# Score pairs in neighbouring PSUM banks, and a new written-out order, in a fused attention and gated-MLP kernel

## The chip, the cores and the metric

The kernel runs on one core of a Trainium2 chip. The metric is the device time of one execution in microseconds (us). Before the change the median of three runs is 380.63 us (377.94 to 382.38). The engines are called PE (TensorE; PEld is its weight load), ACT (ScalarE), DVE (VectorE), POOL (GpSimd) and SP (SyncE, which only issues DMAs here).

## The reference

```
q, k, v: (8 batches, 12 heads, 448 positions, 64)
q_n, k_n = q / rms(q) * g_q, k / rms(k) * g_k          # rms over the 64
attn     = softmax(q_n @ k_n^T / 8)
x        = (attn @ v), heads side by side              # (8, 448, 768)
h        = relu(x @ w_in)                              # 768 -> 1024
u, vv    = h[..., :512], h[..., 512:]
v_n      = (vv - mean(vv)) / sqrt(var(vv) + 1e-6)      # over the 512
v_s      = w_spatial @ v_n + b_spatial                 # mixes the 448 positions
out      = (u * v_s) @ w_out                           # 512 -> 768
```

## The kernel before

The work of one batch is split into three groups of four heads, 24 groups G in all; batch b has the groups 3b to 3b+2. The 448 positions are taken as 7 chunks of 64. Everything is one stream of words in a string `PLAN`; a loop at the end calls for each word the function `op_<letter>`. The order of the words is the order of the instructions on every engine: each engine runs its own instructions in that order and waits by semaphores, which the framework derives from the tiles that instructions read and write. A word has arguments, then after a slash its buffers or banks, then the engine (a ACT, v DVE, g POOL). So `S.13.5/03` computes scores of group 13, unit 5, into banks 0 and 3; `S.13.6/17` unit 6 into banks 1 and 7; `V.3.0.0/2` starts block 0 of batch 3 in bank 2, and `V.3.2.0/6` block 2 in bank 6. All of PSUM is one tile `ps` of 8 banks.

The words, with the lines of the kernel before:

- L, l load raw q or k (SP; l, q, r, i, j, n, p, k are the forms of group 0, cut in halves r so that work starts early); Q squares (L361 POOL or DVE, L359 ACT), R sums (L372, L378), I and J take ln and exp for the reciprocal root (L385, L390; L395, L398), N and n normalise (L404, L412).
- P and p transpose on PE (L426, L435), K and k evict to the tiles qT and kT (L342, L340; kT scaled by the gains, L449 DVE, L447 ACT); T transposes q by DMA instead (L464).
- S computes a pair of score tiles, two banks (L506). E takes exp of both in one ACT instruction into a tile `et` (L514); there are 7 S and 7 E for each group, 168 in all.
- s, a, b are column passes over the `et` tiles (L539): sums of the exps, and the two halves of attn @ v. D and d give the reciprocal sums (L554, L558 ACT), X multiplies into `xt` (L564 DVE).
- V and U are the two halves of x @ w_in (L580, L651); c and u are their relus (L573 DVE, L571 ACT); B takes the statistics (L616, L617), M, m, w prepare them (L622, L625 ACT, L630 DVE), A normalises (L639 ACT); H mixes positions (L665), G multiplies (L670 DVE), O is the output product (L679), W the tails of V and O (L604), o evicts (L342, L340), t writes out (SP, L696).
- v loads v (L290, L293), wi, ws, wo load weights w_in, w_sp, w_out (L300, L304, L307), all on POOL's queue; wb loads the bias on SP (L311). z.44 puts 44 dummy matmuls (L260). gA, gB, gC make the column of gains (L346, L351, L354).

The exp reads its two banks as one stepped slice:

```
act.activation(out=ets[sl[0]], in_=ps[:, a:b + 1:b - a, 0:S], func=AF.Exp, bias=0.0, scale=1.0)
```

In the plan before, b − a is 1 for 40 of the 168 pairs, 2 for 48, and 3 to 7 for 80.

Of the kernel before, what the change touches and what calls it, by code (L numbers as in the profile page):

```python
# [20 lines left out]
l.1.0/0 setup//v l.0.0/1 l.1.1 l.0.1 L.1.0/2 L.1.1/3 L.2.1/4 gA//v L.4.0/5 gB/0 z.44/7 L.2.0/6 q.1.0/0/a r.1.0//v  # L21
q.0.0/1/a r.0.0//v i.0//a j.0//a q.1.1//a q.0.1//g r.1.1//v n.0.0/0/g gC//v r.0.1//v Q.1.0/2/a n.1.0/1/v p.0.0/1
i.1//a p.1.0/2 R.1.0//v j.1//a z.17/7 n.1.1//g Q.1.1/0/a k.0.0/0/v n.0.1//g k.1.0/0/a p.1.1/3 L.3.1/0 R.1.1//v z.8/7
wi.1.0//g L.3.0/1 S.0.0/45 k.1.1//v I.1//a S.0.1/67 J.1//a E.0.0/0/a p.0.1/0 N.1.0/2/v S.0.2/12 E.0.1/1/a N.1.1/3/v
P.1.0/3 L.4.1/2 k.0.1//a z.8/5 K.1.0/1/v Q.2.0/2/g P.1.1/4 L.5.1/3 Q.2.1/1/a z.15/7 K.1.1/1/v E.0.2/2/a R.2.1//v
S.1.0/56 S.1.2/07 v.0.1//g S.0.3/34 E.1.2/3/a S.1.1/12 R.2.0//v v.0.0//g E.1.1/4/a S.1.4/07 Q.3.0/0/v v.0.2//g I.2//a
J.2//a E.1.4/5/a N.2.0/1/v v.0.3//g E.1.0/6/a N.2.1/0/v P.2.0/1 L.5.0/6 E.0.3/7/a S.0.5/02 K.2.0/2/v Q.4.0/1/g
S.1.6/57 E.0.5/8/a P.2.1/6 S.1.3/34 K.2.1/2/v E.1.6/9/a S.0.4/02 z.4/1 Q.3.1/2/v wi.0.1//g E.1.3/a/a S.1.5/57 S.0.6/16
E.1.5/b/a wi.0.3//g s.1.0/3 R.3.1//v a.1.0/4 E.0.6/c/a wi.1.2//g S.2.4/57 R.3.0//v a.1.1 s.1.1 E.2.4/d/a S.2.1/16
s.1.2 R.4.0//v Q.4.1/2/g E.0.4/e/a s.1.3 s.0.0/5 a.0.0/7 I.3//a a.0.1 J.3//a s.0.1 E.2.1/f/a wi.0.2//g s.0.2 R.4.1//v  # L30
s.0.3 D.1/0/a a.0.2 wi.0.0//g S.2.3/02 D.0/1/a N.3.0/2/v S.2.0/16 b.0.0/3 d.0//a b.1.0/5 b.0.1 wi.1.3//g E.2.3/g/a
N.3.1/3/v b.0.2 b.0.3 wi.1.1//g E.2.0/h/a S.2.6/02 X.0.1//v a.0.3 a.1.2 I.4//a X.0.0//v P.3.0/1 J.4//a E.2.6/0/a
N.4.0/1/g S.2.5/36 K.3.0/3/v P.3.1/7 E.2.5/7/a s.2.0/0 K.3.1/3/v a.1.3 S.2.2/12 d.1//a b.1.1 a.2.0/3 Q.5.0/0/g
E.2.2/4/a T.4.0/1 S.3.1/67 b.1.2 E.3.1/6/a b.1.3 S.3.4/12 X.1.1//v a.2.1 E.3.4/1/a L.6.1/4 Q.5.1/1/g X.1.0//v a.2.2
L.7.0/1 S.3.0/67 s.2.1 L.6.0/0 E.3.0/e/a S.3.2/15 b.2.0/4 s.2.2 E.3.2/2/a N.4.1/0/g R.5.1//v s.2.3 S.3.3/26 D.2/1/a
b.2.1 a.2.3 R.5.0//v b.2.2 E.3.3/8/a b.2.3 S.3.6/17 d.2//a S.3.5/05 I.5//a P.4.1/2 X.2.0//v J.5//a V.0.1.0/6 E.3.6/c/a
N.5.0/2/g K.4.1/1/v U.0.3.0/3 E.3.5/3/a V.0.1.1 X.2.1//v U.0.3.1 V.0.1.2 ws//g T.5.0/0 S.4.5/17 c.0.1//v S.4.1/24
E.4.5/a/a W.0/0 N.5.1/3/g B.0.1//v E.4.1/5/a L.7.1/5 S.4.3/56 wb c.0.3//v S.4.4/17 S.4.0/24 E.4.3/b/a U.0.3.2
U.0.2.0/0 Q.7.0/2/a u.0.3//v V.0.0.0/5 B.0.3//v U.0.0.0/6 E.4.4/9/a P.5.1/3 Q.6.0/0/g V.0.0.1 R.7.0//v E.4.0/f/a
U.0.1.0/1 U.0.0.1 Q.6.1/1/a K.5.1/0/v V.0.0.2 v.1.1//g U.0.2.1 c.0.0//a R.6.1//v S.5.2/27 v.1.0//g S.5.3/34 E.5.2/h/a  # L40
U.0.1.1 V.0.2.0/5 R.6.0//v E.5.3/4/a U.0.0.2 V.0.2.1 I.6//a U.0.1.2 J.6//a Q.7.1/2/a V.0.2.2 N.6.0/0/g u.0.1//v
U.0.2.2 u.0.0//v S.5.4/27 S.4.2/34 u.0.2//v E.5.4/g/a Y.1/1 c.0.2//v Y.2/6 v.1.3//g T.6.0/2 E.4.2/7/a R.7.1//v
S.4.6/02 s.3.0/7 N.6.1/1/g E.4.6/d/a s.4.0/5 S.5.0/34 y.2//v s.4.1 L.10.1/2 I.7//a s.3.1 y.1//v s.4.2 J.7//a L.9.0/6
s.3.2 E.5.0/0/a B.0.2//v s.4.3 L.9.1/3 S.5.1/02 v.1.2//g S.5.5/16 D.4/0/a s.3.3 B.0.0//v a.3.0/3 b.3.0/4 D.3/1/a
N.7.0/3/g a.3.1 b.3.1 E.5.5/6/a Y.3/5 P.6.1/7 y.3//v E.5.1/e/a S.5.6/16 K.6.1/2/v Y.0/5 T.7.0/3 M.0//a d.3//a s.5.0/0
y.0//v m.0//a a.5.0/2 E.5.6/2/a b.3.2 w.0//v b.4.0/7 wx//v a.3.2 b.3.3 d.4//a s.5.1 L.8.0/0 a.4.0/5 X.3.1//v A.0.3//a
L.8.1/4 S.6.4/16 a.5.1 Q.10.1/1/g L.10.0/1 A.0.2//a s.5.2 b.4.1 a.3.3 A.0.1//a s.5.3 b.5.0/4 X.3.0//v b.4.2 A.0.0//a
a.4.1 b.5.1 b.4.3 wo//g R.10.1//v E.6.4/8/a a.4.2 a.5.2 b.5.2 a.4.3 N.7.1/2/g a.5.3 D.5/1/a b.5.3 X.4.0//v S.6.1/13
d.5//a S.6.0/06 X.4.1//v H.0.1/5 E.6.1/1/a X.5.1//v H.0.0/7 Q.9.1/0/g E.6.0/3/a L.12.0/5 G.0.1//v P.7.1/4 G.0.0//v
S.6.6/13 K.7.1/3/v H.0.2/5 E.6.6/5/a Q.9.0/2/g X.5.0//v S.7.2/06 S.6.5/47 G.0.2//v S.6.2/13 E.7.2/f/a U.1.3.0/2  # L50
R.9.1//v V.1.2.0/5 Q.8.0/1/g E.6.5/c/a U.1.3.1 R.9.0//v U.1.2.0/0 E.6.2/0/a V.1.0.0/6 U.1.2.1 I.9//a V.1.0.1 J.9//a
Q.8.1/0/a V.1.2.1 N.9.0/1/g U.1.3.2 S.6.3/47 u.1.3//v S.7.4/13 E.6.3/e/a V.1.2.2 U.1.2.2 v.2.0//g c.1.2//v T.9.0/1
E.7.4/7/a V.1.0.2 R.8.1//v S.7.1/24 N.9.1/0/g S.7.3/57 c.1.0//a s.6.0/1 E.7.1/b/a H.0.3/3 R.8.0//v E.7.3/4/a s.6.1
V.1.1.0/6 B.1.0//v v.2.1//g I.8//a P.9.1/2 J.8//a u.1.2//a G.0.3//v s.6.2 N.8.0/3/g S.7.0/45 Q.10.0/2/a K.9.1/1/v
s.6.3 W.1/703 E.7.0/h/a R.10.0//v N.8.1/2/g D.6/0/a T.8.0/0 S.7.6/24 c.1.3//v d.6//a S.9.1/15 V.1.1.1 I.10//a
o.0.3.0/0/v E.7.6/9/a U.1.0.0/7 L.12.1/6 o.0.3.1//v v.2.2//g V.1.1.2 E.9.1/a/a L.11.1/3 U.1.0.1 c.1.1//v L.11.0/0
v.2.3//g S.9.0/02 S.9.4/34 S.7.5/15 E.9.0/6/a B.1.1//v U.1.0.2 Q.12.0/0/g P.8.1/6 E.9.4/g/a O.0.1.0/0 K.8.1/0/v
E.7.5/d/a S.9.6/23 u.1.0//v s.7.0/4 b.6.0/6 J.10//a B.1.3//v s.7.1 o.0.1.0/1/a b.6.1 N.10.0/0/g a.6.0/7 E.9.6/2/a
s.7.2 b.7.0/1 B.1.2//v a.6.1 s.7.3 S.8.3/05 D.7/1/a S.8.0/23 R.12.0//v b.6.2 E.8.3/1/a N.10.1/1/g a.6.2 T.10.0/2
a.7.0/4 b.7.1 a.7.1 M.1//a b.7.2 a.6.3 m.1//a d.7//a a.7.2 b.7.3 X.6.0//v E.8.0/3/a b.6.3 L.14.0/4 v.3.3//g S.8.2/05  # L60
X.6.1//v L.13.1/1 O.0.2.0/7 E.8.2/0/a L.14.1/2 X.7.1//v P.10.1/2 t.0.3 Q.11.1/1/g w.1//v o.0.2.0/2/a a.7.3 K.10.1/2/v
A.1.3//a S.8.1/36 S.9.2/01 S.8.5/57 X.7.0//v E.9.2/e/a O.0.2.1/2 v.3.0//g U.1.1.0/4 E.8.5/8/a o.0.2.1//v O.0.1.1/0
R.11.1//v Q.12.1/2/g E.8.1/c/a U.1.1.1 S.8.4/12 A.1.2//a o.0.1.1//v S.8.6/57 S.10.6/36 E.8.4/b/a O.0.0.0/0 Q.11.0/0/g
R.12.1//v U.1.1.2 E.8.6/h/a O.0.0.1/1 o.0.0.0/3/v I.12//a u.1.1//v b.8.0/2 J.12//a s.8.0/5 A.1.0//a a.8.0/7 N.12.0/2/g
R.11.0//v b.8.1 s.8.1 E.10.6/4/a a.8.1 b.8.2 s.8.2 o.0.0.1//v a.8.2 I.11//a b.8.3 A.1.1//a s.8.3 a.8.3 J.11//a
L.13.0/5 S.10.2/04 D.8/0/a S.10.0/36 N.11.0/3/g H.1.0/1 d.8//a E.10.0/f/a H.1.1/5 X.8.0//v X.8.1//v E.10.2/7/a H.1.3/7
v.3.1//g T.11.0/3 G.1.1//v Q.14.1/1/a V.2.0.0/3 G.1.3//v N.11.1/1/g S.9.5/26 S.10.4/04 G.1.0//v S.10.1/57 E.9.5/d/a
T.12.0/0 V.2.0.1 R.14.1//v H.1.2/1 Q.14.0/2/a Q.13.1/0/g P.11.1/2 E.10.1/5/a G.1.2//v L.15.0/0 V.2.0.2 L.15.1/3
R.14.0//v V.2.1.0/6 E.10.4/9/a W.2/157 N.12.1/0/g K.11.1/3/v Q.13.0/1/a c.2.0//a S.11.6/04 o.1.3.0/0/v I.14//a
U.2.0.0/2 v.3.2//g L.16.1/6 J.14//a c.2.3//v E.11.6/3/a V.2.1.1 t.0.1 U.2.3.0/3 R.13.0//v N.14.0/1/g o.1.3.1//a  # L70
S.10.3/15 S.11.1/04 E.10.3/c/a V.2.1.2 R.13.1//v U.2.3.1 E.11.1/0/a U.2.0.1 N.14.1/3/g B.2.3//v L.16.0/4 P.12.1/7
c.2.1//a U.2.3.2 U.2.0.2 K.12.1/0/v I.13//a J.13//a V.2.2.0/1 u.2.0//a u.2.3//v Q.15.0/2/g S.10.5/05 L.19.0/2
S.11.3/46 S.11.0/27 E.10.5/1/a T.14.0/2 P.14.1/3 V.2.2.1 E.11.3/8/a K.14.1/2/v U.2.1.0/0 N.13.0/2/g V.2.2.2 R.15.0//v
E.11.0/b/a U.2.1.1 S.12.5/35 c.2.2//a B.2.0//v S.12.0/46 b.10.0/2 E.12.5/h/a s.10.0/7 Q.16.1/1/g L.17.1/5 a.10.0/1
B.2.1//v b.10.1 s.10.1 t.1.3 E.12.0/5/a S.12.6/35 t.0.0 s.10.2 B.2.2//v a.10.1 E.12.6/f/a s.10.3 a.10.2 Q.15.1/0/g
b.10.2 a.10.3 D.10/1/a b.10.3 S.9.3/46 S.11.2/35 d.10//a T.13.0/1 O.1.1.0/7 E.11.2/7/a X.10.1//v v.4.2//g U.2.1.2
X.10.0//v E.9.3/c/a O.1.1.1/2 v.4.0//g o.1.1.0/1/v u.2.1//a S.12.3/35 S.11.5/14 o.1.1.1//v S.11.4/67 E.12.3/1/a
Q.16.0/2/g a.9.0/0 R.15.1//v t.1.1 s.9.0/2 a.9.1 E.11.5/9/a s.9.1 a.11.0/3 s.11.0/5 R.16.1//v s.9.2 E.11.4/4/a s.11.1
N.13.1/0/g a.11.1 b.11.0/1 b.9.0/4 R.16.0//v a.9.2 I.15//a M.2//a b.11.1 s.11.2 m.2//a s.9.3 b.9.1 s.11.3 D.9/0/a
a.11.2 b.11.2 L.17.0/1 I.16//a a.9.3 d.9//a a.11.3 b.9.2 J.15//a b.11.3 D.11/1/a X.9.0//v b.9.3 S.14.1/67 w.2//v  # L80
d.11//a U.2.2.0/2 E.14.1/0/a O.1.0.0/5 X.11.0//v Q.17.1/0/g X.11.1//v P.13.1/0 A.2.1//a O.1.0.1/3 o.1.0.0/0/v A.2.2//a
# [657 lines left out]
```

## Time and profile before

| what | value |
|---|---|
| median of 3 runs | 380.63 us (377.94 to 382.38) |
| profiled execution, its own time | 379.37 us |
| its span, first to last instruction | 377.6 us |
| granted TensorE clock, mean | 0.956 |
| busy PE, ACT, DVE, POOL | 78%, 66%, 56%, 40% of the span |
| HBM read, written | 38.55 MB, 11.01 MB |

The span is shorter than the profiled execution's own time, since the latter also holds what lies before the first and after the last instruction. Busy time of PE is modelled with the whole length of each matmul, so that a matmul that starts after a pause counts longer than one in a stream. A row of waits reads: engine and line that waited, who ended the wait, total us, times, the longest us. A row of the timeline reads: start, us, engine, line, operation, out<-in, shapes, count, and in brackets the engine's idle time before it and who ended it.

### The profile page before, as it was taken

What the parts mean: (1) busy time and instruction counts of PE and PEld (TensorE: products, weight loads), DVE (VectorE), ACT (ScalarE), POOL (GpSimd) and SP (SyncE); (2) the same over time, 40 slices, a digit from 0 to 9 for tenths busy, and PEclk for the clock granted to TensorE, in tenths of its full rate; (3) what the DMA queues carried; (4) which work ended last, traced back from release to release, by engine and by line L of the source; (5) the groups of instructions that cost most, each with busy time, mean ns of one, the idle gap of its engine ahead of it and who ended that gap; (6) DMA issues with size and microseconds to landing.
All of it is one profiled execution on the core that took longest, in us unless ns stands there. A gap on an engine that the chain in (4) does not pass through costs nothing. (4 is left out here: it accounts for less than half of the span.)

```text
span 377.6 us, 6689 instructions
## 1 busy us (share of the span) xinstructions
PE 296.3 (78%) x2661; PEld 141.2 (37%) x2661; DVE 209.9 (56%) x340; ACT 248.5 (66%) x383; POOL 151.0 (40%) x123
## 2 busy tenths in 40 slices
PE   4967878877886976976678797888689686879993
PEld 4622323533343342442333243444344232335551
DVE  6884536686576565675566435665362332344672
ACT  5687858755875886866656777678687444675261
POOL 3733670860768278758231534362920040000000
PEclk9976999989999899998999899999999799999998
DMA  7995456890779196967565152618690302030066
GB/s 254 255 226 91 147 106 100 188 272 26 88 182 224 25 197 204 189 126 145 72 158 151 8 120 69 191 19 192 101 137 21 105 1 31 0 107 2 16 182 180
DMA packets 56618, 46.33 MB, mean 123 GB/s; under 512 B 39369, under 2 KB 52170, under 8 KB 56586
## 3 DMA queue, kind: packets, MB, share of 16 engines
q1 hardware_dynamic: 36130, 37.63, 36.2%
q0 software_dynamic: 20448, 8.27, 18.8%
q8 instruction: 21, 0.34, 0.3%
q14 instruction: 11, 0.09, 0.1%
q10 hardware_dynamic: 8, 0.00, 0.0%
HBM read 38.55 MB, written 11.01 MB: 131 GB/s over the span
## 5 line engine op out<-in xcount | busy, mean ns | idle before, releaser
L514 ACT ACTIVATE et<-ps 128x896 bf16<-128x896 f32 x168 | 148.5, 915 | 75.4 <-PE ps L506 22.1
L404 POOL TENSOR_TENSOR nrm<-raw,rs 128x896 bf16<-128x896 f32 x40 | 67.3, 1690 | 110.8 <-ACT rs L390 50.6
L506 PE MATMUL ps<-qT,kT 64*128 64x448 bf16 (+1 forms) x384 | 56.6, 373 | 13.4 <-ACT et L514 12.8
L361 POOL TENSOR_TENSOR sqt<-raw 128x896 f32<-128x896 f32 (+1 forms) x32 | 52.9, 1658 | 32.8 <-DMA raw<-in_q_dram 18.1
L651 PE MATMUL ps<-xt,w_in 128*128 128x448 bf16 x192 | 50.6, 365 | 12.9 <-ACT et L514 12.9
L564 DVE TENSOR_TENSOR xt<-ps,rc 128x448 bf16<-128x448 f32 x48 | 28.3, 619 | 39.5 <-PE ps L539 16.7
L372 DVE TENSOR_REDUCE ss<-sqt 128x14 f32<-128x896 f32 x46 | 48.4, 1076 | 2.2 <-ACT sqt L359 1.5
L539 PE MATMUL ps<-et,vt 128*32 128x448 bf16 x576 | 43.8, 373 | 7.1 <-ACT et L514 7.0
L580 PE MATMUL ps<-w_in,xt 128*128 128x512 bf16 x144 | 41.4, 383 | 8.9 <-ACT et L514 8.9
L679 PE MATMUL ps<-w_out,gt 128*128 128x384 bf16 x192 | 39.2, 337 | 6.9 <-DVE xt L564 2.9
L342 DVE COPY os<-ps 128x384 f32<-128x384 f32 (+1 forms) x43 | 23.3, 555 | 31.8 <-PE ps L679 15.2
L539 PE MATMUL ps<-et,ones 128*32 128x448 bf16 x384 | 33.7, 378 | 3.4 <-ACT et L514 3.3
L506 PEld LDWEIGHTS <-kT 64*128 64x128 bf16 (+1 forms) x384 | 16.0, 98 | 52.6 <-issue 48.8
L665 PE MATMUL ps<-w_spT,vn 128*128 128x448 bf16 (+1 forms) x128 | 29.2, 360 | 5.1 <-ACT et L514 4.8
L651 PEld LDWEIGHTS <-w_in 128*128 128x128 bf16 x192 | 17.6, 99 | 36.1 <-issue 24.0
L639 ACT ACTIVATE vn<-vs,nb,rv 128x512 bf16<-128x512 bf16 (+1 forms) x32 | 24.6, 803 | 9.3 <-DVE nb L630 9.3
L670 DVE TENSOR_TENSOR gt<-ps,us 128x448 bf16<-128x448 f32 x32 | 19.3, 620 | 19.8 <-ACT et L514 10.5
L679 PEld LDWEIGHTS <-gt 128*128 128x128 bf16 x192 | 18.5, 100 | 24.1 <-issue 12.0
L616 DVE BATCH_NORM_STATS2 s<-vs 128x6 f32<-128x512 bf16 (+1 forms) x32 | 21.8, 683 | 5.9 <-ACT vs L571 5.4
L539 PEld LDWEIGHTS <-vt 128*32 128x32 bf16 x576 | 16.2, 98 | 23.6 <-issue 16.7
L573 DVE TENSOR_SCALAR us<-ps 128x448 bf16<-128x448 f32 x20 | 12.2, 619 | 20.4 <-PE ps L651 13.0
L580 PEld LDWEIGHTS <-xt 128*128 128x128 bf16 x144 | 13.2, 98 | 25.2 <-issue 15.4
(70 smaller groups left out, 322.3 us busy)
## 6 DMA issues: line engine op xcount, KB each, us to landing
out_dram<-os SPq DMA_DIRECT2D x56, 192.0 KB, 3.1
raw<-in_q_dram SPq DMA_DIRECT2D x23, 448.0 KB, 5.5
raw<-in_k_dram SPq DMA_DIRECT2D x23, 448.0 KB, 4.7
vt<-in_v_dram POOLq DMA_DIRECT2D x16, 288.0 KB, 5.6
w_in<-in_moe_w_in_dram POOLq DMA_DIRECT2D x8, 192.0 KB, 7.2
vz<-in_v_dram POOLq DMA_DIRECT2D x16, 48.0 KB, 4.6
w_out<-in_moe_w_out_dram POOLq DMA_DIRECT2D x1, 768.0 KB, 12.1
raw<-in_k_dram SPq DMA_DIRECT2D x2, 224.0 KB, 3.4
```

Source lines behind the costliest of these rows:

```text
L361: eng.tensor_tensor(out=t, in0=x, in1=x, op=ALU.mult)
L372: dve.tensor_reduce(out=sss[G % 3][:, i].rearrange("p r c -> p (r c)"), in_=sqt[where.pop(("sq", G, i))].rearrange("p r (c d) -> p (r c) d ...
L404: engines[e or "g"].tensor_tensor(out=nrm[sl[0]].rearrange("p c r d -> p r c d"), in0=raw[where["raw", G, i]].rearrange("p r (c d) -> p r ...
L506: pe.matmul(out=ps[at:at + w, sl[n], 0:S], lhsT=kT[64 * r:64 * r + 64, hh, :, :].rearrange("q c p -> q (c p)")[:, 64 * c:64 * c + w], rhs= ...
L514: act.activation(out=ets[sl[0]], in_=ps[:, a:b + 1:b - a, 0:S], func=AF.Exp, bias=0.0, scale=1.0)
L539: pe.matmul(out=ps[32 * l:32 * l + 32, bank, 0:S], lhsT=w, rhs=et_of(G, l, j), start=(n == 1), stop=(n == 4), tile_position=(0, 32 * l))
L564: dve.tensor_tensor(out=xts[b % 2][:, 2 * g + half, :], in0=ps[:, where.pop(("ab"[half], G))[0], 0:S], in1=rcs[where["rc", G]], op=ALU.mult)
L580: pe.matmul(out=ps[:, bank, :], lhsT=xts[b % 2][:, j, 128 * m:128 * m + 128], rhs=w_in[:, j, DH:], start=(n == 1 and j == 2 * g), stop=(n ...
L639: act.activation(out=y, in_=x, func=AF.Identity, bias=nbs[b % 2][rows, m:m + 1], scale=rvs[b % 2][rows, m:m + 1])
L651: pe.matmul(out=ps[:, bank, 0:S], lhsT=w_in[:, j, 128 * f:128 * f + 128], rhs=xts[b % 2][:, j, :], start=(n == 1 and j == 2 * g), stop=(n ...
L665: pe.matmul(out=ps[:, sl[0], 0:S], lhsT=vns[b % SLOTS["vn"]][rows, m, 128 * f:128 * f + 128], rhs=w_spT[rows, m, :], start=(m == 0), stop= ...
L679: pe.matmul(out=ps[:, sl[0], 0:384], lhsT=gts[b % 2][:, f, 128 * m:128 * m + 128], rhs=w_out[:, f, 384 * h:384 * h + 384], start=(f == 0), ...
```

## The change

Every S word now names two neighbouring banks (b − a is 1 for all 168). The sums, logs and roots of group 0 get tiles of their own with the half r ahead of the index i, and its normalised values get tiles with r ahead of the chunk, so that each instruction of a half writes one whole run; w_in's tile is split into even and odd blocks, so that each of the eight loads writes one whole run of a partition. The order of the words, the banks and the engines of some words are new: 1649 words before and after, the same work. The counts of words whose engine differs:

| word | before | after |
|---|---|---|
| o (output copy) | ACT 21, DVE 43 | ACT 31, DVE 33 |
| u, c (relus) | ACT 12 and 13, DVE 20 and 19 | ACT 7 and 11, DVE 25 and 21 |
| N (normalise) | POOL 40, DVE 6 | POOL 43, DVE 3 |
| Q, q (square) | ACT 13 and 3, POOL 31 and 1, DVE 2 and 0 | ACT 12 and 2, POOL 34 and 2, DVE 0 |
| K, k (evict) | ACT 4 and 2, DVE 22 and 2 | ACT 3 and 1, DVE 23 and 3 |

The start of the plan, and one place further on, before and after:

```diff
-l.1.0/0 setup//v l.0.0/1 l.1.1 l.0.1 L.1.0/2 L.1.1/3 L.2.1/4 gA//v L.4.0/5 gB/0 z.44/7 L.2.0/6 q.1.0/0/a r.1.0//v
-q.0.0/1/a r.0.0//v i.0//a j.0//a q.1.1//a q.0.1//g r.1.1//v n.0.0/0/g gC//v r.0.1//v Q.1.0/2/a n.1.0/1/v p.0.0/1
-i.1//a p.1.0/2 R.1.0//v j.1//a z.17/7 n.1.1//g Q.1.1/0/a k.0.0/0/v n.0.1//g k.1.0/0/a p.1.1/3 L.3.1/0 R.1.1//v z.8/7
-wi.1.0//g L.3.0/1 S.0.0/45 k.1.1//v I.1//a S.0.1/67 J.1//a E.0.0/0/a p.0.1/0 N.1.0/2/v S.0.2/12 E.0.1/1/a N.1.1/3/v
+setup//v l.1.0/0 l.0.0/1 l.0.1 l.1.1 z.50/7 L.1.0/2 L.1.1/3 L.2.0/4 q.1.0/1/a L.2.1/5 r.1.0//v q.0.0/0/g L.3.0/6
+q.0.1//g r.0.0//v q.1.1//a r.0.1//v i.0//a j.0//a r.1.1//v n.1.0//g Q.1.0/2/a n.0.0//v ws//g p.1.0/7 i.1//a j.1//a
+wi.1.3//g R.1.0//v Q.1.1/0/a p.0.0/6 n.1.1//g z.12/5 k.0.0/0/a gA//v R.1.1//v gB/5 n.0.1//g L.3.1/0 z.10/4 Q.2.0/1/a
+wb gC//v p.0.1/4 k.1.0/0/v L.4.1/1 I.1//a p.1.1/5 J.1//a Q.2.1/2/a k.0.1//v N.1.0/0/g S.0.0/01 S.0.2/23 k.1.1//v
+E.0.0/0/a z.3/7 R.2.1//v S.0.3/67 E.0.2/1/a S.0.4/45 N.1.1/1/g L.4.0/2 S.0.6/01 R.2.0//v E.0.3/2/a P.1.0/3 z.7/2
...
-E.13.1/d/a S.13.5/03 o.2.3.0/1/a S.13.6/17 N.15.0/0/g Q.17.0/1/a V.3.0.0/2 o.2.3.1//v V.3.2.0/6 R.17.1//v E.13.6/g/a
-V.3.0.1 V.3.2.1 E.13.5/3/a R.17.0//v v.4.3//g V.3.0.2 T.15.0/3 V.3.2.2 c.3.0//v O.2.1.0/4 N.16.0/2/g I.17//a J.17//a
+o.2.3.0/0/a c.3.3//v P.14.1/5 o.2.3.1//a V.3.2.0/7 K.14.1/3/v E.12.6/g/a V.3.0.1 t.2.3 B.3.3//v V.3.2.1 S.13.6/56
+S.13.0/34 Q.18.1/1/g E.13.6/2/a V.3.0.2 V.3.1.1 E.13.0/h/a c.3.0//v V.3.2.2 V.3.1.2 B.3.0//v J.17//a N.17.1/3/g
...
+    ss0 = const.tile([128, 2, 2, C], FP, name="ss0")
+    ls0 = const.tile([128, 2, 2, C], FP, name="ls0")
+    rs0 = const.tile([128, 2, 2, C], FP, name="rs0")
+    nrm0 = several("nrm0", 2, [128, 2, C, D], BF)
...
-    w_in = const.tile([128, 6, DF], BF, name="w_in")
+    w_in = const.tile([128, 2, NG, DF], BF, name="w_in")
...
-        pool.dma_start(out=w_in[32 * l:32 * l + 32, half::2, :], in_=x)
+        pool.dma_start(out=w_in[32 * l:32 * l + 32, half, :, :], in_=x)
...
-        dve.tensor_reduce(out=sss[0][:, i, r],
+        dve.tensor_reduce(out=ss0[:, r, i],
...
-        act.activation(out=lss[0][:, :, r], in_=sss[0][:, :, r], func=AF.Ln, bias=eps, scale=1.0 / D)
+        act.activation(out=ls0[:, r], in_=ss0[:, r], func=AF.Ln, bias=eps, scale=1.0 / D)
...
-        act.activation(out=rss[0][:, :, r], in_=lss[0][:, :, r], func=AF.Exp, bias=0.0, scale=-0.5)
+        act.activation(out=rs0[:, r], in_=ls0[:, r], func=AF.Exp, bias=0.0, scale=-0.5)
...
-            out=nrm[where["n", 0, i]][:, :, r, :],
+            out=nrm0[i][:, r],
...
-            in1=rss[0][:, i, r].to_broadcast([128, C, D]), op=ALU.mult)
+            in1=rs0[:, r, i].to_broadcast([128, C, D]), op=ALU.mult)
...
-            pe.matmul(out=p_[64 * r:64 * r + 64, 128 * m:128 * m + 128], lhsT=n[:, c, r, :], rhs=ident,
+            pe.matmul(out=p_[64 * r:64 * r + 64, 128 * m:128 * m + 128], lhsT=n[:, r, c, :], rhs=ident,
...
-            pe.matmul(out=ps[:, bank, :], lhsT=xts[b % 2][:, j, 128 * m:128 * m + 128], rhs=w_in[:, j, DH:],
+            pe.matmul(out=ps[:, bank, :], lhsT=xts[b % 2][:, j, 128 * m:128 * m + 128], rhs=w_in[:, j % 2, j // 2, DH:],
```

U and W read w_in by the same new index.

## Prediction

> **What bounds the kernel now.** I first read the head of the page: span, busy shares, granted clock and the chain that ended last.
>
> ```profile
> span 377.6 us, 6689 instructions
> PE 296.3 (78%) x2661; PEld 141.2 (37%) x2661; DVE 209.9 (56%) x340; ACT 248.5 (66%) x383; POOL 151.0 (40%) x123
> PEclk9976999989999899998999899999999799999998
> PE 32%; ACT 13%; DVE 3%; issue 1%; DVEq 0%; ACTq 0%
> ```
>
> No engine is full. The chain is PE and ACT taking turns, which is odd: they should overlap, PE being allowed to run ahead of ACT by several score pairs. So I turned to the list of waits, and looked for these two engines alone.
>
> ```profile
> ACT et L514 <- PE ps L506: 22.1, 33, 1.9
> PE ps L651 <- ACT et L514: 12.9, 17, 1.6
> PE ps L506 <- ACT et L514: 12.8, 19, 1.2
> PE ps L539 <- ACT et L514: 11.8, 15, 1.0
> PE ps L580 <- ACT et L514: 8.9, 11, 1.1
> ACT et L514 <- PE ps L651: 8.4, 10, 1.5
> ACT et L514 <- PE ps L580: 6.0, 8, 1.1
> ACT et L514 <- DVE kT L449: 5.1, 5, 2.0
> ```
>
> Only the first is plain data flow (exp needs its scores). An exp (L514) has no use for U (L651), V (L580) or a kT eviction (L449), nor have U and V for an exp. The timeline shows what joins them:
>
> ```profile
> 190.40 1.04 PE L580 MATMUL ps<-w_in,xt 128*128 128x512 bf16 x4
> 191.47 0.92 ACT L514 ACTIVATE et<-ps 128x896 bf16<-128x896 f32 x1 [0.77 <-PE ps L580]
> 192.44 1.02 PE L580 MATMUL ps<-w_in,xt 128*128 128x512 bf16 x4 [1.00 <-ACT et L514]
> 193.07 0.92 ACT L514 ACTIVATE et<-ps 128x896 bf16<-128x896 f32 x1 [0.68 <-PE ps L580]
> 194.04 1.02 PE L580 MATMUL ps<-w_in,xt 128*128 128x512 bf16 x4 [0.57 <-ACT et L514]
> ```
>
> By the plan, these exps are E.13.6 (scores in banks 1 and 7) and E.13.5 (banks 0 and 3), and the matmuls are V.3.0 in bank 2 and V.3.2 in bank 6. The scores of both were written by 190.45. E.13.6 starts a microsecond later, when the V matmuls in the banks *between* 1 and 7 end; V.3.0 then waits for each exp whose pair spans bank 2. An exp that reads banks a and b by a stepped slice is ordered as if it used all banks from a to b.
>
> I tested that on all 168 exps, laying the plan's words beside the records in order, by the distance b−a and the ACT idle time ahead of the exp:
>
> ```
> distance            1     2     3     4     5     6     7
> exps               40    48    19    22    20    14     5
> mean idle, us    0.10  0.33  0.44  0.68  0.73  0.87  1.02
> ```
>
> The exp's own duration is the same at every distance (0.91 to 0.92 us). From the other side, PE idles 61.6 us in waits that an exp ended; in 76 of them, 58.2 us, the matmul's bank is not one of the exp's two and it reads none of that exp's output.
>
> Last, the stages: before the first exp, the exps, and behind the last.
>
> ```profile
> 0.00:13.78 13.78, 8.92 (x96) 8.03 (x96) 9.20 (x28) 7.06 (x13) 6.11 (x12) 1.00 0.84 283
> 13.78:337.70 323.92, 253.52 (x2318) 115.12 (x2316) 181.22 (x275) 224.94 (x339) 144.86 (x112) 0.95 0.57 120
> 337.70:377.60 39.90, 33.84 (x252) 18.07 (x251) 19.43 (x38) 16.47 (x32) 0.00 (x0) 0.97 0.32 90
> ```
>
> Columns after the length: busy PE, PEld, DVE, ACT, POOL, then clock, DMA share, GB/s. In the middle ACT idles 99.0 us of 323.9, PE 70.4.
>
> **The change, part by part.**
>
> *Neighbouring banks.* All 168 pairs become neighbours, so the slice has no middle. The 128 wide pairs hold 71.4 us of idle time (the table: 48×0.33+19×0.44+22×0.68+20×0.73+14×0.87+5×1.02), 0.56 each. At the 0.10 of the 40 that are neighbours already, 128×0.46 = 58.4 us go. The PE count, 58.2, is the same stall seen from its other end, so it counts once. In the built program's list of instructions, exps that wait for DVE fall from 63 to 17. What is late next: exps then wait for their own scores, which is data flow.
>
> *Restarts of PE.* A matmul after a stall takes its whole 0.36 us, in a stream 0.19 per step, so 76 stalls cost 76×0.17 = 13 us that count as busy. Bounds 0 and −13: it pays only where PE sets the pace. PE's share of the chain is 32%, so −4.2.
>
> *Waits that the pairs bring.* A pair now needs two free neighbours of eight, so it more often follows an exp that empties the same banks. By the plans, S words behind their immediate predecessor's exp rise from 24 to 29, behind the last but one they fall from 79 to 66. An S that waits for the exp just ahead leaves ACT idle for hand-over, scores and hand-over: 0.05 (V at 192.44 after the exp's end at 192.39), 0.36 (L506), 0.05, so 0.46: 5×0.46 = +2.3. Queued behind the waiting S on PE are column passes and U/V matmuls, then DVE's evictions of them. If the 66 paid it too, +30: the upper bound.
>
> *The order and the engines.* Counted from the plans: ACT takes 10 more output copies (0.488), 5 fewer relus of u (0.537), 2 fewer of c (0.593), two fewer squares (0.94 and 0.55) and two fewer q/k evictions (some 0.95): −2.4 us. DVE loses 10 copies (0.557), 3 normalisations (1.214) and 2 squares (1.44), gains 5 and 2 relus (0.619, 0.686) and 2 evictions (0.68): −6.3. POOL gains three normalisations (1.690), three squares (1.658) and a half square (0.93): +11.0, to 162 us, still only half busy. ACT's −2.4 lies between 0 and −2.4 on the path: −1.0. DVE and POOL I cost at nothing: both keep over 100 us idle; the cover is gone in the first 14 exps, where the new plan gives POOL some 19 us of work against ACT's 21; that part stands among the rivals. Behind the last exp the words of both plans hold PE work that differs by about 1 us: nothing.
>
> *The start.* The warm-up matmuls (44, 4.88 us from 5.37) sat behind the gain product and held the first transposes to 10.18; 50 now come first, from when the identity is ready (1.6 us), done by 7.2. Then the chain square, reduce, ln/exp, normalise ends n.0.1 on POOL at about 11.0, two transposes and an eviction later the first exp could start at 12.8: −1.0. Against it, the w_sp load (392 KB; before issued at 51.45) now goes on POOL's queue ahead of the first w_in load and of n.1.1, while DMA is at 0.84, and two more full squares (0.95 each) stand on ACT ahead of the first exp and need the third and fourth whole load, which share the engines with w_sp: 392 KB at 283 GB/s is 1.4 us, twice that if the float32 side counts. So −1.0 to +2.5; I take +0.5. The bias load moves forward on SP ahead of L.4.1: 1.8 KB, nothing, since that load waits for its buffer.
>
> *Small tiles and w_in.* The same bytes and operations at other addresses. The most that could be a needless wait there is the idle time ahead of L412, 0.7 us, which ACT's rs ended: 0 to −0.7, taken as 0. The first U and V run at 50 us, long after the w_in loads.
>
> [...] This row is odd:
>
> ```profile
> L630 DVE SCALAR_TENSOR_TENSOR nb<-mv,rv 128x4 f32<-128x4 f32 x8 | 11.4, 1424 | 6.6 <-ACT rv L625 6.6
> L617 DVE BATCH_NORM_AGGREGATE mv<-s 128x2 f32<-128x6 f32 (+1 forms) x32 | 5.8, 180 | 1.1
> ```
>
> Sixteen bytes per partition take 1.42 us. [...]
>
> *Sum.* 377.6 − 58.4 − 4.2 + 2.3 − 1.0 + 0.5 = 316.8 of span. The profiled execution took 379.37, 1.8 more than its span, and the median is 380.63, 1.3 more again: 319.9, say 320.
>
> **The rivals.**
>
> *ACT packs better.* The new order may fill ACT beyond what the removed waits give. For: all 13 us of restarts, and the clock: granted 0.956, so at most 0.044×377.6×0.78 = 13 us of PE time is lost to slow stretches, half of which denser matmuls might win back. Against: with 222 us of work in a middle stage of some 264 ACT would already be at 84%. 320 − 8.8 − 6.5 − 1.5 = 303.
>
> *Pairs wait for pairs.* Bank pairs are scarce, and POOL is tight at the start: the 66 S words pay too, 320 + 30 = 350. For: waits of S matmuls on ACT rise from 69 to 126 in the built program. Against: today such true waits are 2.3 us in 6 cases.
>
> *Ping-pong takes over (slower).* If nearly every S stood behind the exp ahead of it, 168×0.46 = 77 us would come back: 320 + 77 = 397. It decides from 61/0.46 = 132 of the 168 pairs. The plan's 29 speak against.
>
> *The banks between were not the cause.* If the order comes from the whole PSUM tile rather than its span, nothing falls away: 380. Against: the table's first column.
>
> **How the numbers follow.** Forecast (304 to 335) 0.67; ACT packs better (below 304) 0.09; pairs wait for pairs (335 to 370) 0.18; no cause 0.03; ping-pong 0.03. Below 303 and above 349 I leave out some 0.08 and 0.10. Within 1%, about what a measurement of this kernel can tell from no change, 0.03; slower 0.03; faster 0.94.
>
> **What would show it.** Right: in the list of waits PE's rows on L651, L580, L665 against exp fall to a few us, ACT's idle time ahead of the exp from 75 to about 20 us, mostly ended by the score matmuls, and ACT's middle stage near 264 us. The first exp stands between 12.8 and 16.3. Wrong: score matmuls waiting for exps by more than 30 us in all, or an idle time ahead of exps as before.

## The result, and the profile after

The changed kernel takes 304.44 us (median of four runs, 303.11 to 307.02), against 381.5 us before: 0.800 of it, with an interval of 0.791 to 0.808. The profiled execution has a span of 303.9 us, where the forecast's sum had 316.8. Here are the lines of the page that answer to those shown of before:

```profile
span 303.9 us, 6670 instructions
PE 279.4 (92%) x2649; PEld 134.9 (44%) x2661; DVE 200.0 (66%) x334; ACT 240.3 (79%) x382; POOL 162.3 (53%) x130
PEclk9799699999999999999997999979999999999998
PE 74%; DMA 8%; POOL 5%; issue 4%; ACT 3%; DVE 2%; SPq 1%; POOLq 0%; DVEq 0%; ACTq 0%
```

PE is busy 92% of the span, and the chain is PE for three quarters, with ACT at 3%. The turn-taking has gone. In the list of waits only two rows that name the exp (now L517) and PE or DVE are left among the nearly sixty longest:

```profile
ACT et L517 <- PE ps L509: 16.9, 30, 4.2
DVE xt L567 <- ACT et L517: 1.7, 1, 1.7
```

The exp waits for its own scores. All the rows in which U, V or the column passes stood against an exp are gone, and of the evictions one output copy behind an exp is left, 0.7 us. Ahead of the exps ACT idles 18.3 us in all, 75.4 before; PE idles 1.2 us in waits that an exp ended, 61.6 before. The stages (windows before the first exp, of the exps, and behind the last; columns as in the prediction):

```profile
0.00:14.64 14.64, 10.04 (x106) 9.07 (x106) 10.26 (x28) 8.08 (x15) 7.68 (x14) 0.88 0.87 253
14.64:265.77 251.13, 237.30 (x2300) 108.71 (x2313) 170.54 (x269) 216.13 (x337) 154.62 (x117) 0.97 0.76 154
265.77:303.90 38.13, 32.08 (x253) 17.15 (x246) 19.21 (x38) 16.14 (x31) 0.00 (x0) 0.98 0.38 105
```

The middle stage fell from 323.9 to 251.1 us, 72.8 less; start and tail moved by 0.9 and −1.8. (Some executions took some two per cent longer with the same program, one each of e1, e4 and e8 below and four of the six of e7: the ratios leave them out, the medians do not, the traces of e4 and e7 are of such executions, and the other two of e7 took 302.9 and 305.1 us.)

### The profile page after: what moved, and what is told of

Same layout as the page of the kernel before. It is cut to its first block, busy times and chain, and to the rows that moved or that the text cites. A ratio compares the mean times of both kernels' runs of the same rounds, so it can differ in the third digit from the quotient of the medians.

```text
span 303.9 us, 6670 instructions
## 1 busy us (share of the span) xinstructions
PE 279.4 (92%) x2649; PEld 134.9 (44%) x2661; DVE 200.0 (66%) x334; ACT 240.3 (79%) x382; POOL 162.3 (53%) x130
## 4 chain that ended last, share of the span: by engine, by line
PE 74%; DMA 8%; POOL 5%; issue 4%; ACT 3%; DVE 2%; SPq 1%; POOLq 0%; DVEq 0%; ACTq 0%
PE ps L542 18%; PE ps L509 12%; PE ps L654 11%; PE ps L682 10%; PE ps L668 9%; PE ps L583 8%; DMA vt<-in_v_dram 4%; PE ps L607 4%; DMA raw<-in_k_dram 3%; PE ps L429 2%; POOL nrm L408 2%; ACT et L517 1%; POOL sqt L365 1%; POOL nrm L415 1%; ACT vn L642 1%
## 5 line engine op out<-in xcount | busy, mean ns | idle before, releaser
L517 ACT ACTIVATE et<-ps 128x896 bf16<-128x896 f32 x168 | 146.7, 918 | 18.3 <-PE ps L509 16.9
L408 POOL TENSOR_TENSOR nrm<-raw,rs 128x896 bf16<-128x896 f32 x43 | 72.7, 1700 | 41.2 <-ACT rs L394 32.6
L365 POOL TENSOR_TENSOR sqt<-raw 128x896 f32<-128x896 f32 (+1 forms) x36 | 58.8, 1643 | 25.4 <-DMA raw<-in_k_dram 8.8
L509 PE MATMUL ps<-qT,kT 64*128 64x448 bf16 (+1 forms) x384 | 53.9, 361 | 3.9 <-DVE kT L452 3.0
L542 PE MATMUL ps<-et,vt 128*32 128x448 bf16 x576 | 43.6, 377 | 4.5 <-DMA vt<-in_v_dram 4.5
L654 PE MATMUL ps<-xt,w_in 128*128 128x448 bf16 x192 | 46.4, 354 | 0.4
L583 PE MATMUL ps<-w_in,xt 128*128 128x512 bf16 x132 | 37.0, 380 | 0.8 <-ACT os L344 0.3
L682 PE MATMUL ps<-w_out,gt 128*128 128x384 bf16 x192 | 36.2, 326 | 0.1
L346 DVE COPY os<-ps 128x384 f32<-128x384 f32 (+1 forms) x33 | 18.0, 554 | 13.0 <-PE ps L682 8.8
L654 PEld LDWEIGHTS <-w_in 128*128 128x128 bf16 x192 | 16.6, 98 | 19.9 <-issue 7.4
L576 DVE TENSOR_SCALAR vs<-ps 128x512 bf16<-128x512 f32 (+1 forms) x21 | 14.4, 684 | 11.2 <-PE ps L583 7.6
L344 ACT ACTIVATE os<-ps 128x384 f32<-128x384 f32 (+1 forms) x31 | 14.6, 489 | 8.0 <-PE ps L682 5.9
```

Source lines behind the costliest of these rows:

```text
L365: eng.tensor_tensor(out=t, in0=x, in1=x, op=ALU.mult)
L408: engines[e or "g"].tensor_tensor(out=nrm[sl[0]].rearrange("p c r d -> p r c d"), in0=raw[where["raw", G, i]].rearrange("p r (c d) -> p r ...
L509: pe.matmul(out=ps[at:at + w, sl[n], 0:S], lhsT=kT[64 * r:64 * r + 64, hh, :, :].rearrange("q c p -> q (c p)")[:, 64 * c:64 * c + w], rhs= ...
L542: pe.matmul(out=ps[32 * l:32 * l + 32, bank, 0:S], lhsT=w, rhs=et_of(G, l, j), start=(n == 1), stop=(n == 4), tile_position=(0, 32 * l))
L583: pe.matmul(out=ps[:, bank, :], lhsT=xts[b % 2][:, j, 128 * m:128 * m + 128], rhs=w_in[:, j % 2, j // 2, DH:], start=(n == 1 and j == 2 * ...
L654: pe.matmul(out=ps[:, bank, 0:S], lhsT=w_in[:, j % 2, j // 2, 128 * f:128 * f + 128], rhs=xts[b % 2][:, j, :], start=(n == 1 and j == 2 * ...
```

## The experiments

All ratios are to the kernel before, run on the same chip in the same rounds, with 95% intervals (e1 to e4 on one chip, e5 to e8 on a second, e9 on a third).

| run | what differs | median us | ratio | span us | PE idle in waits for an exp, us (waits) |
|---|---|---|---|---|---|
| before | | 381.5 | 1 | 377.6 | 61.6 (85) |
| after | | 304.4 | 0.800 (0.791 to 0.808) | 303.9 | 1.2 (5) |
| e1 | old order, all pairs neighbours | 303.2 | 0.792 (0.788 to 0.797) | 300.9 | 1.3 (7) |
| e2 | new order, 130 pairs wide | 372.5 | 0.973 (0.967 to 0.978) | 370.7 | 54.0 (80) |
| e3 | new order, 31 pairs wide | 338.3 | 0.884 (0.879 to 0.890) | 336.3 | 35.0 (34) |
| e9 | before, each exp in two | 312.3 | 0.817 (0.812 to 0.822) | 310.0 | 0.4 (5) |
| e5 | after, scores twice | 326.8 | 0.857 (0.851 to 0.862) | 327.0 | 0.3 (1) |
| e6 | after, exp and a copy | 307.1 | 0.804 (0.798 to 0.810) | 306.4 | 2.9 (13) |
| e4 | after, w_sp late | 305.3 | 0.797 (0.793 to 0.802) | 307.1 | 1.8 (7) |
| e7 | e1, warm-up first | 308.7 | 0.797 (0.790 to 0.804) | 307.0 | 1.1 (7) |
| e8 | after, old layouts | 301.9 | 0.790 (0.784 to 0.795) | 299.9 | 1.4 (5) |

**Which part of the change did it? e1, e2.** The change put pairs into neighbouring banks and at the same time wrote a new order with jobs on other engines. e1 keeps everything of the kernel before and deals out the banks anew; 395 bank entries of the string differ, and nothing else:

```diff
-S.13.5/03 ... S.13.6/17 ... V.3.0.0/2 ... V.3.2.0/6
+S.13.5/34 ... S.13.6/56 ... V.3.0.0/7 ... V.3.2.0/0
```

> The order and the engines of the plan before, tile layouts of before; only the banks are dealt out anew, so that all 168 score pairs are neighbours. Pairs theory: the false waits and the restarts of PE go, 58.4 + 13 us, as if nothing else had been changed: 381 - 71 = 310 us, 302 to 322. Order theory (the gain came from the new order and the moved jobs): 360 to 381 us.

It took 303.2 us. The place that the prediction showed, E.13.6 and E.13.5 among the V passes of batch 3, now reads as follows (timeline of e1; the rows of other engines, of the weight loads and of a square on ACT are left out):

```profile
155.11 2.76 PE L580 MATMUL ps<-w_in,xt 128*128 128x512 bf16 x12
...
156.26 1.73 ACT L514 ACTIVATE et<-ps 128x896 bf16<-128x896 f32 x2
...
157.71 0.81 PE L679 MATMUL ps<-w_out,gt 128*128 128x384 bf16 x4
```

All twelve V matmuls in one stretch, 2.76 us where they took from 190.40 to 195.06, and both exps back to back beside them, once ACT has done a square. In e1's waits, ACT behind its scores is 12.2 us, PE's S behind an exp 0.9:

```profile
ACT et L514 <- PE ps L506: 12.2, 25, 1.4
DVE kT L449 <- ACT et L514: 1.7, 3, 1.2
PE ps L506 <- ACT et L514: 0.9, 2, 0.5
```

e2 is the converse: the plan after with its banks renamed, so that order, engines, bank reuse and every true wait stay. (Where the renaming turns a pair round, the exp reads it in rising order and the passes take the other half of `et`.)

```diff
-S.13.5/67 ... V.3.0.0/0 ... V.3.2.0/7 ... S.13.6/56
+S.13.5/37 ... V.3.0.0/2 ... V.3.2.0/7 ... S.13.6/53
```

> The plan after, with its eight banks renamed (2,0,6,1,4,5,3,7 for 0 to 7), so that order, engines, bank reuse and so every true wait stay, and 130 of the 168 pairs are wide: 44 at distance 2, 19 at 3, 31 at 4, 26 at 5, 10 at 6. By the table of before these bring 75 us of idle time ahead of the exps instead of 17. Pairs theory: 304 + 58 + 13 = 375 us, 355 to 390. Order theory: 304 to 315 us.

372.5 us. The page's group of the exp in e2:

```profile
L519 ACT ACTIVATE et<-ps 128x896 bf16<-128x896 f32 x168 | 150.8, 915 | 83.1 <-PE ps L509 45.7 <-PE ps L543 7.4 <-PE ps L655 5.6
```

Idle ahead of the exps is back at 83 us, with one exp still 0.915 us long. That makes four corners: with neighbours the old order takes 303 us and the new one 304, with wide pairs the old one 382 and the new one 372. So the whole gain came from the pairs: e1 has all of it without the new order. With neighbours the new order with its moved jobs brought nothing that these runs can tell from zero, since the intervals of e1 and of the change overlap. With wide pairs it is 9 us the faster, beyond the interval of e2; but its wide pairs lie at other distances, and PE waits 54 us for exps where it waited 62, so that these runs can't say how much of the 9 us is the order's own.

**How much for each wide pair? e3.** Renaming the banks in a ring makes wide pairs of one kind only, 0 and 7, and 31 of them.

```diff
-S.13.5/67
+S.13.5/70
```

> The plan after with its banks renamed in a ring (bank 7 becomes 0, all others one more), so that the 31 pairs of banks 6 and 7 become pairs of 0 and 7, which span everything; the other 137 stay neighbours. Pairs theory: 31 x (1.02 - 0.10) = 28 us and some 40 restarts of 0.17, 7 us: 339 us, 325 to 350. Order theory: 304 us. If PE's restarts cost nothing, 332 at most, and the loss equals the growth of PE's idle time by the profile; if they count in full, the loss is that growth plus 0.17 for each new stall.

338.3 us, 339 expected. The idle time of PE in waits for exps grew by 33.8 us in 29 more waits, over one microsecond each. The expectation held a test of whether PE's restarts count, and it does not decide: those waits alone grew by as much as the time did (33.8 us by the medians), but other waits shrank meanwhile, and all idle time of PE grew by only 22.0.

**Is it the banks or the instruction? e9.** Banks far apart might be bad in themselves. e9 leaves them where they were and issues each exp as two instructions, one for each bank.

```diff
-        act.activation(out=ets[sl[0]], in_=ps[:, a:b + 1:b - a, 0:S], func=AF.Exp, bias=0.0, scale=1.0)
+        for n, bank in enumerate((a, b)):
+            act.activation(out=ets[sl[0]][:, n, :], in_=ps[:, bank, 0:S], func=AF.Exp, bias=0.0, scale=1.0)
```

> The kernel before with nothing moved: same order, same engines, same banks, 128 wide pairs. Only each exp is issued as two, one for each bank, so that no instruction's slice has a middle. ACT pays for it: 448 columns take some 0.54 us (the Ln of a 128x448 tile, L554), 168 x (2 x 0.54 - 0.92) = 27 us more. Span theory (the order comes from the one instruction's slice): all false waits go, 303 us as with the old order in neighbouring banks, plus 2 to 10 us since PE sets the pace and not ACT: 305 to 313 us. Rival (banks far apart are bad in themselves, or the scarce banks of this order): 370 us or more.

312.3 us. Its exps and its waits:

```profile
L515 ACT ACTIVATE et<-ps 128x448 bf16<-128x448 f32 x336 | 156.3, 562 | 12.1 <-PE ps L506 11.5
ACT et L515 <- PE ps L506: 11.5, 21, 1.6
DVE os L342 <- ACT et L515: 1.2, 1, 1.2
```

No PE row against an exp is left, with 128 pairs still wide. It is the stepped slice of one instruction that ties up the banks between. Each half takes 0.562 us, so ACT pays 168 × (2 × 0.562 − 0.915) = 35 us more work, and the span is only 9.1 us longer than e1's.

**Who sets the pace now? e5, e6.** The forecast took a third of PE's restarts into its sum because ACT seemed to become the tighter engine. e5 gives PE more to do, e6 ACT.

```diff
-        for r, hh, c, w, at, n in todo:
+        for r, hh, c, w, at, n in todo + todo:
```

> The plan after; each score word issues its matmuls twice into the same banks (the second writes the same values over the first), so PE gets 168 x 0.19 = 32 us more streamed work, all of it ahead of the last exp, and nothing else. If PE sets the pace (which is why its restarts counted in full): 304 + 26 to 32 = 330 to 336 us. If ACT sets it, as the forecast held when it took a third of the restarts: 304 + 5 to 15 = 309 to 319 us.

```diff
         act.activation(out=ets[sl[0]], in_=ps[:, a:b + 1:b - a, 0:S], func=AF.Exp, bias=0.0, scale=1.0)
+        act.activation(out=spare[(7 * G + u) % 4], in_=spare_in, func=AF.Copy, bias=0.0, scale=1.0)
```

> The plan after; each exp is followed on ACT by a copy of 16 values per partition into a spare tile that nobody reads, some 0.2 us, so ACT gets 168 x 0.2 = 34 us more. If PE sets the pace and ACT idles a fifth: 304 + 5 to 15 = 309 to 319 us. If ACT sets it: 330 to 338 us.

The chain of e5, its wait of exps for scores, and the group of the copy that e6 adds:

```profile
PE 90%; DVE 4%; ACT 1%; issue 1%; DMA 1%; POOL 1%; SPq 0%; ACTq 0%; DVEq 0%; POOLq 0%
```

```profile
ACT et L517 <- PE ps L509: 43.6, 68, 4.8
```

```profile
L521 ACT ACTIVATE spare<-spare_in 128x16 f32<-128x16 f32 x168 | 37.7, 224 | 0.0
```

In e5 PE was busy 30.9 us longer, and the span grew by 23.1 us; the exps' wait for scores rose from 16.9 to 43.6 us, and the chain is PE for 90%. In e6, 37.7 us more for ACT lengthened the span by 2.6 us, no more than runs of one kernel differ, and less than the 5 to 15 us that were expected. PE sets the pace; ACT took its added work into idle time. e5 fell short of its 26 to 32: PE's remaining idle time, 18.6 us up to its last matmul, shrank to 10.9 and paid for part.

**The start: e4, e7, e8.** In the trace after, the largest single wait of PE is for a v tile, 4.5 us at 31.2 (the next, 3.4 us at 162.2 and 3.0 at 198.8, have their like in e4, e6 and e8, and no run tried to remove them). The w_sp load and the first w_in load, issued at 9.12 and 9.81 us, had gone ahead of it. e4 moves them behind the v loads.

```diff
-... n.0.0//v ws//g p.1.0/7 i.1//a j.1//a wi.1.3//g R.1.0//v ...
+... n.0.0//v p.1.0/7 i.1//a j.1//a R.1.0//v ... wi.0.1//g wi.1.3//g ... wi.1.0//g ws//g ...
-... Y.1/0 ... y.1//v ... y.3//v ...
+... y.3//v Y.1/4 y.1//v ...
```

> The plan after with the w_sp load and the first w_in load moved behind the v loads of batch 0 (and the transposes of w_sp behind their three sisters, in another bank). Theory: the two early loads hold up the v tiles, for which PE waits 4.5 us at 31.2; without them the v tiles land before the column passes, 299 to 301 us, the first exp at 14.0 to 14.6. Rival: the v tiles are late because all DMA engines are full then, whatever the order; 303 to 305 us with the same wait.

The wait for the v tile went (they landed at 24.1 and 25.8 us in place of 29.8 and 31.1), and the time did not move (305.3 us, where 299 to 301 were expected without the wait). Between the first exp and the 29th the two traces need nearly the same time, 36.8 us after and 36.1 in e4: others had come in place of the one wait, and PE's waits of over 0.3 us in this stretch still sum to 3.1 us, 4.9 after. e7 moves the warm-up matmuls ahead of the gain product in e1.

```diff
-gA//v L.4.0/5 gB/0 z.44/1 L.2.0/6
+gA//v L.4.0/5 z.44/1 gB/0 L.2.0/6
```

> The old order with all pairs in neighbouring banks, and one word moved: the 44 warm-up matmuls go ahead of the gain product, as in the plan after, so they run from 1.7 to 6.6 us and not from 5.6. Theory: they no longer hold the first transposes back, the first exp starts 0.5 to 1.5 us earlier, 301.7 to 302.7 us. Rival: the first exp stands where the raw loads let it, 303 us.

The first exp started at 13.7 us, 0.4 earlier than in e1, a little less than expected; the comparison shows no gain (0.797 against e1's 0.792). e8 undoes the layouts.

```diff
-        pool.dma_start(out=w_in[32 * l:32 * l + 32, half, :, :], in_=x)
+        pool.dma_start(out=w_in[32 * l:32 * l + 32, half::2, :], in_=x)
...
-        dve.tensor_reduce(out=ss0[:, r, i],
+        dve.tensor_reduce(out=ss0[:, i, r],
...
-            out=nrm0[i][:, r],
+            out=nrm0[i][:, :, r, :],
```

> The plan after, with the small tiles of group 0 and w_in laid out as before (index i ahead of the half r, chunk ahead of r, w_in's blocks interleaved), so that a half or a load writes a stepped piece. Forecast's term: 0 to 0.7 us lost, 304 to 305 us. Rival: needless waits at the start, as with the pairs, several us: 307 us or more.

301.9 us, under what either theory said: the old layouts cost nothing that can be told. Stepped slices of these SBUF tiles did not bring microseconds of waits as stepped slices of the PSUM tile did; the runs do not say why. Six traces with the same words at the start (after, e2, e3, e5, e6, e8) have their first exp at 14.2 to 16.6 us, so a term of 1 us at the start is below what one trace can show. e8's ratio of 0.790 is the lowest of all, but its interval overlaps that of the change, as do those of e1, e4 and e7: no run is shown to be faster than the change.

## Why the prediction was right, point by point

The measured 304.4 us lies inside the range of 303 to 349, near its lower end; 320 was 5% too high. It also lies 0.4 us above the line between the forecast's band (304 to 335) and that of "ACT packs better" (below 304), and the change's own runs go from 303.1 to 307.0: on which side it fell is luck. What the steps said, and what came:

- *Neighbouring banks, −58.4 us.* Right in cause and size. PE's idle time in waits for exps fell by 60.4 us here and by 60.3 in e1, with the order unchanged; ACT's ahead of the exps fell by 57.1 and 61.5. (The products that the prediction writes out come to 71.0 and 58.9; its 71.4 and 58.4 are the unrounded means.)
- *Restarts of PE, 0 to −13, taken as −4.2.* PE's busy time fell by 16.9 us, which holds this term and the clock's. The size was off: this is the main term that was mis-sized. PE's share of the old chain was no measure of who would set the pace once the waits were gone. e5 and e6 show that PE does, so what the restarts cost counts in full: all of the 13 us, if the estimate of 0.17 us for each (0.36 for a whole score matmul less 0.19 from start to start in a stream, both from the trace before) is right, 9 more than was taken.
- *The slow clock, 0 in the sum.* The second mis-sized term; it stood only with the rival that ACT packs better. The granted clock rose from 0.956 to 0.969, and fell to 0.937 and 0.945 in e2 and e3. The other executions go the same way: of those that the ratios use, 0.941 to 0.957 before, 0.933 to 0.954 in e2 and e3, and 0.955 to 0.991 with neighbouring pairs or split exps. So an idler PE was also a slower PE here: its lost time, (1 − clock) × span, is 16.6 us before, 9.0 in e1, 9.4 after, 23.4 in e2, 18.5 in e3.

These three terms close the sum within 2.5 us in four pairs of traces. Of the lost clock time I count 0.8, PE's rough busy share (78% before), and 0.17 us for each wait:

```
                 span     PE idle, all   restarts      clock          sum
before to after -73.7       -56.7      80 x -0.17   0.8 x  -7.2     -76.1
before to e1    -76.7       -58.6      78 x -0.17   0.8 x  -7.6     -78.0
after to e2     +66.8       +42.4      75 x +0.17   0.8 x +14.0     +66.4
after to e3     +32.4       +22.0      29 x +0.17   0.8 x  +9.1     +34.2
```

The idle time is read from the traces; the two other terms are estimates, and only their sum can be checked. PE's busy time fell by 16.9 us to after and by 18.3 to e1, where the two give 19.4 each, and rose by 24.7 to e2 and by 10.5 to e3, where they give 24.0 and 12.2.

In the clock records of before and after, the granted clock is 1.0 or 0.5 and nothing between: 32.9 us of the span at half rate before, 18.8 after, and 46.4 in e2. In e2 no two matmuls lay more than 1.84 us apart, and its clock, 0.937, was the slowest of all traces.

```profile
PEclk9565998999989869999999999999998999999998
```

How much of the half-rate time the waits for exps brought is less sure. Of e2's 46.4 us, 24 lie in the first 38 us, where e5, e6 and e8, with the same words and neighbouring pairs, had 13.7; from 40 us to the last exp e2 has 20.5, before also 20.5, after and e1 6.8. In e9, where no exp held PE up, 13.7 us of this stretch ran at half rate, around other waits of 2.9 to 4.3 us.

- *Waits that the pairs bring, +2.3.* Not there: PE waited 1.2 us for exps in all, 61.6 before, and its score matmuls only 0.5 us, in two waits. An S that takes over the banks of an exp just ahead seldom held PE up.
- *Order and engines, −1.0; POOL's +11 and DVE's −6.3 at nothing.* e1 against the change: nothing measurable. ACT's −2.4 could not have counted, since ACT has slack (e6).
- *The start, +0.5 within −1.0 to +2.5.* The first exp came at 14.64, 0.9 later than before; the same start gave up to 16.6 in other runs. What I had not foreseen is that the moved load would show as a wait for v, and in e4 the time did not fall without it.
- *The odd row, nb.* It took 0.90 us in the mean after (1.42 before), with POOL busy 62% of the middle stage (45% before); its longest took 3.55 us. The ACT wait behind it fell from 9.3 to 5.0 us. Its long times fall together with work of POOL. In before, after and e1 the eleven nb instructions with no POOL instruction beside them took 0.15 to 0.17 us, the thirteen with one 0.29 to 4.81 us, and each of these ended within 0.04 us of the end of a POOL instruction. One of them, 3.55 us long, lasted through several POOL instructions in a row, and PE paid for it (timeline of after; rows in between are left out):

```profile
194.57 3.55 DVE L633 SCALAR_TENSOR_TENSOR nb<-mv,rv 128x4 f32<-128x4 f32 x1
194.77 1.68 POOL L365 TENSOR_TENSOR sqt<-raw 128x896 f32<-128x896 f32 x1
196.41 1.68 POOL L408 TENSOR_TENSOR nrm<-raw,rs 128x896 bf16<-128x896 f32 x1
198.04 0.67 DVE L452 TENSOR_SCALAR kT<-ps,g_col 128x896 bf16<-128x896 bf16 x1
198.77 0.68 PE L509 MATMUL ps<-qT,kT 64*128 64x448 bf16 x6 [3.01 <-DVE kT L452]
```

The kT eviction stands behind nb on DVE, and PE waits 3.0 us for that eviction. In e1 the nb of 4.81 us stands in the same way ahead of a PE wait of 4.2 us. So what nb costs hangs here on which POOL work it happens to meet; POOL's busy share of the middle stage rose from 45% to 62% while nb's mean fell from 1.42 to 0.90 us.

Of the rivals, "ACT packs better" named the right leftovers (restarts and clock, 303 us) and gave them to the wrong engine: ACT has idle time to spare, and it is PE that came closer to being busy all through (92% of the span, 78% before). "Pairs wait for pairs" and "ping-pong" did not occur, and e1, e2 and e9 exclude that the banks between were not the cause.

Of what was to show it: PE's rows against exps fell below the few us, the idle time ahead of exps came to 18 us where 20 were said, the middle stage to 251 us where 264 were, and the first exp stood at 14.64 us, within its bounds.

## What to carry to other kernels

When two engines take turns in the chain though their data do not make them, look at what one instruction's slice spans, not at what it reads: a stepped slice over one big tile can tie up all that lies between, as here, where PE idled 61.6 us in waits for exps before and 1.2 us with neighbouring banks. Sort the waiting instruction by that span (here the distance of its two banks) and see whether its idle time grows with it; if it does, rename the buffers before the order is searched anew, since the renaming was the whole gain here. And when a stall goes, add to its idle time the restart of the engine that waited (estimated here at 0.17 us for each wait) and the clock that it lost (granted 0.956 before, 0.969 after), in full, if that engine then sets the pace; which engine that will be, its share of the old chain does not tell. A few small instructions with long means, such as nb here (1.42 us before, 0.15 to 0.17 with no POOL instruction beside it), are worth a look one by one.

## What the runs showed of the hardware that was not expected

The granted clock was lower with many short waits: e2, with 80 waits for exps of at most 1.84 us each, 54 us in all, had 0.937 and 46.4 us at half rate, where e1 with 1.3 us of such waits had 0.970 and 17.8. A DVE instruction of 0.16 us on two SBUF tiles took up to 4.81 us beside POOL, through several POOL instructions in a row. An exp over two banks took, in the trace before, 0.91 to 0.92 us whether the banks were neighbours or seven apart, and split in two it cost 0.21 us more (0.562 for each half).
